# Value products of a token tile in one matmul run, and block outputs written into a dead input tile

## The chip, the cores and the metric

The kernel runs on one core of a Trainium2 chip. The metric is the device time of one execution in microseconds (us). Where several runs are shown, their median counts.

## The reference: what is computed

Two stages follow each other. The first is attention with 8 batches, 8 heads, 512 local and 32 global tokens and a head width of 64. A local token looks at the 32 tokens on either side of it and at the global tokens; a global token looks at all 544. The second is a two-layer network over the 4352 resulting rows of 512 numbers, with 2048 hidden units.

```
s_ll = scale * q_l @ k_l.T, masked to |i-j| <= 32;  s_lg = scale * q_l @ k_g.T
out_l = softmax([s_lg, s_ll]) @ [v_g, v_l]
out_g = softmax(scale * q_g @ [k_g, k_l].T) @ [v_g, v_l]
x = [out_g, out_l], one row of 512 for each token
h = x @ w_in;  g = h / (1 + exp(-h));  result = g @ w_out
```

The weights arrive in 64-bit floats and are decoded on the chip.

## The kernel before, in words

**Steps and tiles.** A step, numbered k from 0 to 127, handles 128 local tokens of one batch and two heads (u = 0, 1). Four steps (the index `pr`, 0 to 3, which stands for pairs of heads) make a token tile of 128 tokens by 512 columns. Four tiles (the index c, 0 to 3) make a batch. There are 32 such tiles, and two more hold the global rows of four batches each.

**A step.** `st_load` and `st_vload` fetch queries with keys (`raw`) and values (`vraw`). `st_scores` makes the scores of both heads in PSUM (`s`), and VectorE and ScalarE turn them into probabilities (`probs`). These have to be transposed into `pt`. For k under 24 TensorE transposes them (`t`), and ScalarE copies the result. From k = 24 on, GpSimd splits the words into halves (`st_halves`), a DMA writes them to DRAM (`st_away`), and a transposing DMA brings them back into `pt` (`st_back`). `st_turn` also lets GpSimd copy the columns of the global probabilities into `pt`. `st_out` then makes the value products: four matmuls in fp32, each appearing in the trace as two records. The values of 128 rows by 64 columns are the stationary operand, `pt` streams 128 or 160 columns, and the two heads use the two column halves of the array. One PSUM bank (`o`) takes the result of a step. ScalarE rounds it into `xh`, VectorE writes the remainder into `xl`, and a third instruction adds the partial sums of the global rows to `acc`.

**The first 28 steps** score with one fp32 matmul for each head. It uses 64 rows of the array, and each head writes a bank of its own. Later steps split their operands into high and low parts, and both heads share a bank.

**The network.** The 34 tiles are grouped into 12 blocks (`SIZES`), ten of three tiles and two of two. For a block `n` and a slice `f` of 128 hidden units (16 of them), `first_layer` makes 12 matmuls into `h` from `xh`, `xl` and the weights, ScalarE and VectorE turn that into `gh` and `gl`, and `second_layer` adds nine matmuls (three for each tile) to the banks `out`. After the last slice ScalarE copies these banks to tiles named `o`, two buffers in rotation, from which the results leave by DMA.

**The order of the work.** TensorE's order is that in which the program is written. Every part of a step gets a time in steps relative to its score (`DUE`, and `DMAT` from k = 24 on): the parts are sorted by it into one stream, and `fill` lets the stream advance a little after each piece of the network. So the attention steps of block n+1 are spread over the matmuls of block n. Before block 0 there is nothing to fill, and its twelve steps run alone. The queue of SyncE (SP) takes DMAs in the stream's order from k = 28 on. A scheduler orders the other engines.

**Buffers that matter.** `pt` has 3, `vraw` 4, `halves` 1, and the copies in DRAM (`planes`) 2. Outside the start, three PSUM banks rotate over scores, transposes and value products.

Of the kernel before, what the change touches and what calls it, by code (L numbers as in the profile page):

```python
# [16 lines left out]
ALU = mybir.AluOpType  # L17
# [19 lines left out]


SIZES = (3,) * 10 + (2, 2)
BUFS = dict(qk=2, raw=2, p=2, vraw=4, halves=1, pt=3)  # L40
ND = 28
KF = 24
GF = 3
# [3 lines left out]
FIRSTW = {2: 1, 3: 1, 4: 1, 5: 1, 6: 1, 7: 1, 8: 1, 9: 1, 10: 1, 11: 1}  # L47
JOINS, SPLITS = (9.0, 9.6, 10.2, 10.8, 11.4, 12.0), (12.1, 12.7)

FIRST = dict(load=(-1.2, -1.1, -1.0, 0.1), vload=(-0.9, 0.2, 0.3, 1.1), turn=(3.2, 4.0, 4.9, 5.8), out=(4.3, 5.2, 6.1, 7.0),  # L50
             gload=(1.2, 2.2, 3.2, 3.3), gscores=(3.4, 4.2, 5.1, 6.0), gsoft=(4.4, 6.2), gturn=(6.9, 8.0),
             late=8.5, then=7.3)

DUE = dict(load=-1.2, split=-0.5, vload=-0.6, turn=1.6, out=2.2)
DMAT = dict(vload=2.2, halves=0.7, away=1.05, turn=1.3, back=1.65, out=3.4)
HEAD = dict(load=-0.6, split=0.2, scores=0.8, soft=1.0, slot=0.3)
HEADS0, HEADS = (11, 1), (7, 2)
TURN1, TURN = (0.65, 1.5), (0.4, 1.5)
# [4 lines left out]
def attention_moe_kernel(ctx: ExitStack, tc: tile.TileContext, qk0_in, qk_in, v_in, gqk, wts, out):  # L63
    nc = tc.nc
# [3 lines left out]
    work = ctx.enter_context(tc.tile_pool(name="work", bufs=1))  # L68
    two = ctx.enter_context(tc.tile_pool(name="two", bufs=2))
    small = ctx.enter_context(tc.tile_pool(name="small", bufs=4))  # L70
    planes = ctx.enter_context(tc.tile_pool(name="planes", bufs=2, space=bass.MemoryType.DRAM))
    ps_att = ctx.enter_context(tc.tile_pool(name="ps_att", bufs=1, space=PSUM))
    ps_h = ctx.enter_context(tc.tile_pool(name="ps_h", bufs=2, space=PSUM))
    ps_out = ctx.enter_context(tc.tile_pool(name="ps_out", bufs=1, space=PSUM))
# [92 lines left out]
    def fetch_weights():  # L167
        i = w_next[0]
        w_next[0] += 1
        f, half = divmod(i, 2)  # L170
        if half and f >= SCRATCH:
            homes_ = [work.tile([P, QW + KW], I32, tag="qk", bufs=BUFS["qk"], name=f"raw_w{i}_{q}")[:, :DM] if f % 2
                      else two.tile([P, DM], I32, tag="o", name=f"raw_w{i}_{q}") for q in range(2)]
        else:
            taken.add(f + SCRATCH * half)
            homes_ = [scratch(f + SCRATCH * half, I32, f"raw_w{i}")]
        n = DM // len(homes_)
        w_raw.append([(raw, q * n, n) for q, raw in enumerate(homes_)])
        for raw, c0, n in w_raw[i]:
            hold(nc.sync.dma_start(out=raw, in_=wts[f, :, DM * half + c0 : DM * half + c0 + n].bitcast(I32)))  # L180
# [111 lines left out]
    tiles = {}  # L292
# [27 lines left out]
    def st_scores(k, b, c, pr):  # L320
        if k < ND:
            raw = tiles.pop(("raw", k))
        else:
            qk, klo = tiles.pop(("qk", k))
        if k < ND:
            ss = [attbank("s", f"s{k}_{u}")[:, :W] for u in range(2)]
            for u in range(2):
                rows = slice(D * u, D * (u + 1))
                nc.tensor.matmul(ss[u], raw[rows, P * u : P * (u + 1)], raw[rows, QW : QW + W], start=True, stop=True)  # L329
        else:  # L330
            s = attbank("s", f"s{k}")
            ss = [s[:, u * W : (u + 1) * W] for u in range(2)]
            for u in range(2):
                q, ks = qk[:, u * P : (u + 1) * P], slice(u * W, (u + 1) * W)
                nc.tensor.matmul(ss[u], q, qk[:, QW:][:, ks], start=True, stop=False)  # L335
                nc.tensor.matmul(ss[u], q, klo[:, ks], start=False, stop=True)  # L336
# [12 lines left out]
        nc.vector.tensor_scalar(out=p[:, 1, :W], in0=p[:, 1, :W], scalar1=st[:, 7:8], scalar2=None,  # L349
                                op0=ALU.mult)  # L350
        tiles["p", k] = p.rearrange("p u j -> p (u j)")
# [36 lines left out]
            src = pgu[SG * pr : SG * (pr + 1), :].rearrange("p (u q) -> p u q", u=2)  # L388
            nc.gpsimd.tensor_copy(out=pt[:SG, :, 1, P:], in_=src)

    def st_out(k, b, c, pr, t):
        n, i = block_of[t]
        xh, xl = xtiles(n)
        sl = slice(i * P, (i + 1) * P)
        vraw, pt = tiles.pop(("vraw", k)), tiles.pop(("pt", k))
        if k < NPR:
            tiles["late", k] = vraw
        o = attbank("o", f"o{k}")
        wide = P + SG
        for a in range(2):  # L400
            m = wide if (a == 0 or c == NC - 1) and k >= NPR else P
            for u in range(2):
                nc.tensor.matmul(o[D * u : D * (u + 1), :m], vraw[:, a, u, :], pt[:, u, a, :m], start=(a == 0),  # L403
                                 stop=(a == 1))
        nc.scalar.copy(out=xh[:, pr, sl], in_=o[:, :P])
        nc.vector.tensor_tensor(out=xl[:, pr, sl], in0=o[:, :P], in1=xh[:, pr, sl].bitcast(F32), op=ALU.subtract)  # L406
        if k >= NPR:
            gdst = acc[:, pr, SG * (b % 4) : SG * (b % 4 + 1)]
            if c == 0 and k >= NST:
                nc.vector.tensor_copy(out=gdst, in_=o[:, P:wide])  # L410
            else:
                nc.vector.tensor_tensor(out=gdst, in0=o[:, P:wide], in1=gdst, op=ALU.add)
# [30 lines left out]

    def xtiles(n):
        if n not in xblk:
            xblk[n] = tuple(two.tile([P, NPR, 3 * P], F32R, tag=f"x{j}", name=f"x{j}_{n}") for j in "hl")
        return xblk[n]


# [3 lines left out]
    def put(when, fn, *a):  # L453
        stream.append((when, fn, a))

    AHEAD = NPR
    for k, (t, b, c, pr) in enumerate(steps):
# [102 lines left out]
    def second_layer(n, f, gh, gl):  # L560
        if f == 0:
            outs[n] = [ps_out.tile([P, DM], F32, tag=f"out{i}", name=f"out{n}_{i}") for i in range(SIZES[n])]
        wh, wl = w_hi[f][:, DM:], w_lo[f][:, DM:]

        last = n + 1 == len(SIZES) and f == NF - 1
        for i in (reversed(range(SIZES[n])) if last else range(SIZES[n])):
            o = outs[n][i]
            sl = slice(i * P, (i + 1) * P)
            nc.tensor.matmul(o, gh[:, sl], wh, start=(f == 0), stop=False)  # L569
            nc.tensor.matmul(o, gh[:, sl], wl, start=False, stop=False)  # L570
            nc.tensor.matmul(o, gl[:, sl], wh, start=False, stop=(f == NF - 1))  # L571
# [103 lines left out]
```

## Time and profile before

| | |
|---|---|
| median of three runs | 1020.04 us (1017.97 to 1020.83) |
| the profiled execution | 1017.49 us |
| its span, first to last instruction | 1015.7 us |
| granted TensorE clock, mean | 0.989 |
| TensorE matmul busy | 990.8 us (98%) |
| VectorE, ScalarE, GpSimd busy | 632.2, 586.7, 236.6 us |

In the profile, PE is TensorE's matmuls, PEld its weight loads, DVE is VectorE, ACT is ScalarE, POOL is GpSimd and SP is SyncE. A row of the timeline gives the start, the duration, the engine, the line of the kernel, the operation, what is written from what, and the shapes. `128*64` means 128 rows and 64 columns of the array. Matmuls are pipelined, so their durations overlap: what a matmul costs is read from the distance between the starts of neighbours.

### The profile page before, as it was taken

How to read it: one execution, taken by the hardware profiler on the slowest of the kernel's cores; microseconds unless marked ns; L12 is line 12 of the kernel's file. 1: busy time of each engine (PE TensorE's matmuls, PEld its weight loads, DVE VectorE, ACT ScalarE, POOL GpSimd, SP SyncE). 2: the span in 40 equal slices, each digit the busy share in tenths (PEclk: the TensorE clock that was granted, in tenths of full speed). 3: DMA queues.
4: the chain of work that ended last, by engine and by line, in shares of the span. 5: the costliest groups of instructions: out<-in, count | busy, mean ns of one | idle time of the engine just before them, and what ended most of it. 6: DMA issues, size and time to landing. Idle time of an engine off the chain costs nothing.

```text
span 1015.7 us, 17864 instructions
## 1 busy us (share of the span) xinstructions
PE 990.8 (98%) x5792; PEld 838.9 (83%) x5792; DVE 632.2 (62%) x1977; ACT 586.7 (58%) x1549; POOL 236.6 (23%) x420
## 2 busy tenths in 40 slices
PE   7899899999999999999999999999999999999998
PEld 4567667888888888888888888888888888888896
DVE  4678874666776577755577667766677665543332
ACT  7788665565756655654566555665566555443332
POOL 2153432223222222211222212221222221110000
PEclk9799999999999999999999999999999999999999
DMA  8683525667665675544475567566766665432000
GB/s 302 205 289 130 158 84 146 163 161 179 187 167 152 176 172 151 166 116 121 119 176 164 145 188 173 145 171 161 172 148 169 158 171 141 121 93 63 1 22 21
DMA packets 177116, 151.05 MB, mean 149 GB/s; under 512 B 117376, under 2 KB 137344, under 8 KB 177024
## 3 DMA queue, kind: packets, MB, share of 16 engines
q1 hardware_dynamic: 172800, 142.32, 51.8%
q10 hardware_dynamic: 4224, 7.60, 2.2%
q8 instruction: 46, 0.75, 0.3%
q14 instruction: 46, 0.38, 0.1%
HBM read 86.44 MB, written 36.18 MB: 121 GB/s over the span
## 4 chain that ended last, share of the span: by engine, by line
PE 90%; DVE 4%; ACT 3%; issue 1%; POOL 0%; DVEq 0%; ACTq 0%; POOLq 0%
PE h L547 36%; PE out L569 13%; PE out L570 12%; PE out L571 12%; PE o L403 8%; PE s L335 2%; PE s L336 2%; DVE w L201 1%; PE s L329 1%; DVE raw_w L200 1%; PE gs L245 1%; PE t L377 1%; PE gt L283 1%; ACT w L198 1%; ACT w_hi L210 1%
## 5 line engine op out<-in xcount | busy, mean ns | idle before, releaser
L547 PE MATMUL h<-xh,w_hi 128*128 128x384 f32 (+1 forms) x768 | 255.8, 333 | 0.5 <-DVE st L340 0.5
L547 PE MATMUL h<-xl,w_hi 128*128 128x384 f32 (+1 forms) x768 | 251.7, 328 | 0.6 <-DVE xl L406 0.6
L547 PE MATMUL h<-xh,w_lo 128*128 128x384 f32 (+1 forms) x768 | 252.1, 328 | 0.0
L569 PE MATMUL out<-w_hi,gh 128*128 128x512 f32 x544 | 225.7, 415 | 0.5 <-ACT gh L556 0.4
L553 ACT ACTIVATE t<-h 128x384 f32<-128x384 f32 (+1 forms) x192 | 90.6, 472 | 221.0 <-PE h L547 203.5
L571 PE MATMUL out<-w_hi,gl 128*128 128x512 f32 x544 | 214.1, 394 | 3.8 <-DVE gl L557 3.8
L570 PE MATMUL out<-w_lo,gh 128*128 128x512 f32 x544 | 214.3, 394 | 0.0
L359 POOL COPY halves<-probs 128x512 uint16<-128x512 uint16 x208 | 141.3, 704 | 243.0 <-DVE probs L349 122.2
L554 DVE SCALAR_TENSOR_TENSOR t<-t,h 128x384 f32<-128x384 f32 (+1 forms) x192 | 101.8, 530 | 105.5 <-ACT t L553 104.2
L547 PEld LDWEIGHTS h<-xh,w_hi 128*128 128x128 f32 x768 | 145.1, 189 | 13.1 <-issue 6.2
L557 DVE TENSOR_TENSOR gl<-t,gh 128x384 fp32r<-128x384 f32 (+1 forms) x192 | 106.5, 555 | 77.3 <-PE out L571 64.8
L344 ACT ACTIVATE probs<-probs,st 128x224 f32<-128x224 f32 x244 | 116.2, 477 | 60.9 <-DVE st L340 59.3
L547 PEld LDWEIGHTS h<-xl,w_hi 128*128 128x128 f32 x768 | 145.2, 189 | 6.7 <-DVE xl L406 0.9
L547 PEld LDWEIGHTS h<-xh,w_lo 128*128 128x128 f32 x768 | 144.9, 189 | 0.0
L340 DVE CUSTOM_DVE_ANT_0 probs<-s,mask 128x224 f32<-128x224 f32 x244 | 86.7, 387 | 87.4 <-PE s L336 73.4
L556 ACT CAST gh<-t 128x384 fp32r<-128x384 f32 (+1 forms) x192 | 94.7, 493 | 59.3 <-DVE t L554 57.7
L569 PEld LDWEIGHTS out<-w_hi,gh 128*128 128x128 f32 x544 | 102.6, 189 | 31.1 <-issue 12.5
L571 PEld LDWEIGHTS out<-w_hi,gl 128*128 128x128 f32 x544 | 102.3, 188 | 28.5 <-DVE gl L557 5.4
L386 POOL COPY pt<-pgt 128x64 f32<-128x64 f32 x124 | 37.4, 302 | 370.9 <-PE o L403 292.5
L570 PEld LDWEIGHTS out<-w_lo,gh 128*128 128x128 f32 x544 | 103.0, 189 | 11.2
L403 PE MATMUL o<-pt,vraw 128*64 128x160 f32 x992 | 92.6, 307 | 4.9 <-issue 3.4
L403 PEld LDWEIGHTS o<-pt,vraw 128*64 128x64 f32 x992 | 60.2, 138 | 41.5 <-issue 33.1
(85 smaller groups left out, 1171.9 us busy)
## 6 DMA issues: line engine op xcount, KB each, us to landing
raw<-in_qk_dram SPq DMA_DIRECT2D x100, 352.0 KB, 3.4
away<-halves SPq DMA_DIRECT2D x104, 256.0 KB, 2.1
vraw<-in_v_dram SPq DMA_DIRECT2D x124, 128.0 KB, 3.1
raw_w<-in_wts_dram SPq DMA_DIRECT2D x24, 512.0 KB, 4.7
raw_g<-in_gqk_dram SPq DMA_DIRECT2D x32, 304.0 KB, 3.7
out_dram<-o ACTq DMA_DIRECT2D x28, 256.0 KB, 2.4
raw<-in_qk_dram SPq DMA_DIRECT2D x28, 240.0 KB, 3.1
raw_w<-in_wts_dram SPq DMA_DIRECT2D x16, 256.0 KB, 3.3
```

Source lines behind the costliest of these rows:

```text
L340: nc.vector.tensor_tensor_reduce(out=p[:, u, :W], in0=ss[u], in1=mask_of[c], scale=-SCALE, scalar=3.0e38, op0=ALU.add, op1=ALU.min, accum_ ...
L344: nc.scalar.activation(p[:, u, :W], p[:, u, :W], AF.Exp, bias=st[:, u : u + 1], scale=-1.0, accum_out=st[:, 2 + u : 3 + u])
L359: nc.gpsimd.tensor_copy(out=halves[:, :, u], in_=p[:, 2 * P * u : 2 * P * (u + 1)].bitcast(U16).rearrange("p (j h) -> p h j", h=2))
L403: nc.tensor.matmul(o[D * u : D * (u + 1), :m], vraw[:, a, u, :], pt[:, u, a, :m], start=(a == 0), stop=(a == 1))
L547: nc.tensor.matmul(h[:, :nt], wt, x[:, c, :nt], start=(i == 0), stop=(i == 3 * NCC - 1))
L553: nc.scalar.activation(t[:, :nt], h[:, :nt], AF.Tanh, scale=0.5)
L554: nc.vector.scalar_tensor_tensor(out=t[:, :nt], in0=t[:, :nt], scalar=1.0, in1=h[:, :nt], op0=ALU.add, op1=ALU.mult)
L556: nc.scalar.copy(out=gh[:, :nt], in_=t[:, :nt])
L557: nc.vector.tensor_tensor(out=gl[:, :nt], in0=t[:, :nt], in1=gh[:, :nt].bitcast(F32), op=ALU.subtract)
L569: nc.tensor.matmul(o, gh[:, sl], wh, start=(f == 0), stop=False)
L570: nc.tensor.matmul(o, gh[:, sl], wl, start=False, stop=False)
L571: nc.tensor.matmul(o, gl[:, sl], wh, start=False, stop=(f == NF - 1))
```

## The change: what it does

- `st_out` is called once for a tile instead of once for a step. It makes the value products of the tile's four steps one behind another, two steps in each of two PSUM banks. Each bank is then evicted with one ScalarE copy, one VectorE subtraction and one VectorE addition to `acc`, over twice the columns.
- Its time is 3.2 steps after the last of the four scores (2.2 for k under 24, and 7.0 on the stream's own scale for the first tile). Before, each step had its own at 3.4 (2.2).
- `pt` has 4 buffers and `planes` 3. The loads of values, the turns and the transposing DMAs of a tile's first steps get later times (`FIRST4`, `DMAT4`), so that they stand behind the run of the tile before.
- The scores of the first 28 steps use all 128 rows and one bank for both heads (`raw` is zero in the other head's rows).
- The `o` tiles go. The results of block n are copied into one tile that takes the place of the block's own `xh`, and leave from there. Two small weight staging buffers move to the tags `o` and `halves`, with one buffer each.

```
-BUFS = dict(qk=2, raw=2, p=2, vraw=4, halves=1, pt=3)
+BUFS = dict(qk=2, raw=2, p=2, vraw=4, halves=1, pt=4)
-FIRST = dict(load=(-1.2, -1.1, -1.0, 0.1), vload=(-0.9, 0.2, 0.3, 1.1), turn=(3.2, 4.0, 4.9, 5.8), out=(4.3, 5.2, 6.1, 7.0),
+FIRST = dict(load=(-1.2, -1.1, -1.0, 0.1), vload=(-0.9, 0.2, 0.3, 1.1), turn=(3.2, 4.0, 4.9, 5.8), out=7.0,
-DMAT = dict(vload=2.2, halves=0.7, away=1.05, turn=1.3, back=1.65, out=3.4)
+DMAT = dict(vload=1.5, halves=0.7, away=1.05, turn=1.3, back=1.65, out=3.2)
+FIRST4 = (dict(vload=1.25), dict(vload=0.3))
+DMAT4 = (dict(vload=2.25, turn=2.3, back=2.4),)
...
-            ss = [attbank("s", f"s{k}_{u}")[:, :W] for u in range(2)]
-                nc.tensor.matmul(ss[u], raw[rows, P * u : P * (u + 1)], raw[rows, QW : QW + W], start=True, stop=True)
+        s = attbank("s", f"s{k}")
+        ss = [s[:, u * W : (u + 1) * W] for u in range(2)]
+                nc.tensor.matmul(ss[u], raw[:, qs], raw[:, QW : QW + W], start=True, stop=True)
...
-    def st_out(k, b, c, pr, t):
+    def st_out(k0, b, c, t):
+        for pr in range(NPR):
+            k = k0 + pr
+            vraw, pt = tiles.pop(("vraw", k)), tiles.pop(("pt", k))
+            if pr % 2 == 0:
+                banks_.append(attbank("o", f"o{k}"))
+            o = banks_[-1][:, wide * (pr % 2) : wide * (pr % 2 + 1)]
...
+        for i, o in enumerate(banks_):
+            prs = slice(2 * i, 2 * i + 2)
+            o = o[:, : 2 * wide].rearrange("p (r q) -> p r q", r=2)
+            hi = xh[:, prs, sl]
+            nc.scalar.copy(out=hi, in_=o[:, :, :P])
+            nc.vector.tensor_tensor(out=xl[:, prs, sl], in0=o[:, :, :P], in1=hi.bitcast(F32), op=ALU.subtract)
+            if k0:
+                gdst = acc[:, prs, SG * (b % 4) : SG * (b % 4 + 1)]
...
-        put(at + due["out"], st_out, *a, t)
+        if pr == NPR - 1:
+            put(at + due["out"], st_out, k - pr, b, c, t)
...
+            done_ = work.tile([P, 3 * DM], F32, tag=f"xh{n % 2}", name=f"o{n}")
-                    sb = two.tile([P, DM], F32, tag="o", name=f"o{n}_{i}")
+                sb = done_[:, DM * i : DM * (i + 1)]
```

The first place is TensorE inside block 2 of the network, at the value products of steps 40 to 43. `o40` is the bank, `pt1` the transposed probabilities, `vraw40` the values, `out2_1` an output bank of block 2, `gs` the scores of global tokens. Before, step 40 stands alone:

```order
L570 MATMUL out2_1_3006<-w_lo4_900,gh2_4_3178 128x512
L571 MATMUL out2_1_3006<-w_hi4_899,gl2_4_3179 128x512
L403 MATMUL o40_3286<-pt1_127,vraw40_3203 64x160 x2
L403 MATMUL o40_3286<-pt1_127,vraw40_3203 64x128 x2
L569 MATMUL out2_2_3007<-w_hi4_899,gh2_4_3178 128x512
L570 MATMUL out2_2_3007<-w_lo4_900,gh2_4_3178 128x512
```

Now the four steps stand together:

```order
L252 MATMUL gs1_3_3_3381<-klo_g3_3_3343,qk_g3_3_3342 128x272
L408 MATMUL o40_3391<-pt0_126,vraw40_3096 64x160 x2
L408 MATMUL o40_3391<-pt0_126,vraw40_3096 64x128 x2
L408 MATMUL o40_3391<-pt1_127,vraw41_3121 64x160 x2
L408 MATMUL o40_3391<-pt1_127,vraw41_3121 64x128 x2
L408 MATMUL o42_3400<-pt2_128,vraw42_3207 64x160 x2
L408 MATMUL o42_3400<-pt2_128,vraw42_3207 64x128 x2
L408 MATMUL o42_3400<-pt3_129,vraw43_3279 64x160 x2
L408 MATMUL o42_3400<-pt3_129,vraw43_3279 64x128 x2
L583 MATMUL out2_1_2894<-w_hi8_1184,gh2_8_3309 128x512
```

Before, the steps 40 to 43 stood one by one in the pieces of slices 4, 5, 7 and 8 of block 2. The first three moved back to the fourth, in slice 8.

The second place is SP's queue at the same steps. `away` is the write of the halves to DRAM, the row with `DMA_TRANSPOSE` brings them back. Before:

```order
L364 DMA away40_3098<-halves40_3070 128x1024
L299 DMA raw42_3100<-in_qk_dram 128x704
L368 DMA_TRANSPOSE pt1_127<-away40_3098 128x4x256
L364 DMA away41_3191<-halves41_3143 128x1024
L299 DMA raw43_3193<-in_qk_dram 128x704
L307 DMA vraw40_3203<-in_v_dram 128x256
L368 DMA_TRANSPOSE pt2_128<-away41_3191 128x4x256
```

Now:

```order
L364 DMA away40_3000<-halves40_2960 128x1024
L302 DMA raw42_3002<-in_qk_dram 128x704
L364 DMA away41_3089<-halves41_3018 128x1024
L302 DMA raw43_3091<-in_qk_dram 128x704
L310 DMA vraw40_3096<-in_v_dram 128x256
L368 DMA_TRANSPOSE pt0_126<-away40_3000 128x4x256
L310 DMA vraw41_3121<-in_v_dram 128x256
L368 DMA_TRANSPOSE pt1_127<-away41_3089 128x4x256
L221 DMA raw_g3_2_3144<-in_gqk_dram 128x608
L364 DMA away42_3177<-halves42_3151 128x1024
L302 DMA raw44_3179<-in_qk_dram 128x704
```

The way back of step 40 moved behind the way out of step 41 and behind the load of the values of step 40; the load of `raw44` now follows two such pairs.

The third place is TensorE just ahead of block 0, where nothing else fills the engine. `t11` are the transposes of step 11, `h0_0` is the first matmul of the network. Before:

```order
L377 MATMUL t11_647<-ident_88,probs__118 128x128 x4
L245 MATMUL gs0_1_1_664<-raw_g1_1_607 64x272
L245 MATMUL gs1_1_1_667<-raw_g1_1_607 64x272
L403 MATMUL o11_670<-pt2_128,vraw11_555 64x160 x2
L403 MATMUL o11_670<-pt2_128,vraw11_555 64x128 x2
L329 MATMUL s13_0_685<-raw13_645 128x224
L329 MATMUL s13_1_686<-raw13_645 128x224
L547 MATMUL h0_0_702<-xh_0_233,w_hi0_618 128x384
```

Now:

```order
L377 MATMUL t11_596<-ident_88,probs__118 128x128 x4
L248 MATMUL gs0_1_1_611<-raw_g1_1_565 64x272
L248 MATMUL gs1_1_1_614<-raw_g1_1_565 64x272
L408 MATMUL o8_617<-pt0_126,vraw8_488 64x160 x2
L408 MATMUL o8_617<-pt0_126,vraw8_488 64x128 x2
L408 MATMUL o8_617<-pt1_127,vraw9_490 64x160 x2
L408 MATMUL o8_617<-pt1_127,vraw9_490 64x128 x2
L408 MATMUL o10_626<-pt2_128,vraw10_492 64x160 x2
L408 MATMUL o10_626<-pt2_128,vraw10_492 64x128 x2
L408 MATMUL o10_626<-pt3_129,vraw11_524 64x160 x2
L408 MATMUL o10_626<-pt3_129,vraw11_524 64x128 x2
L333 MATMUL s13_650<-raw13_594 128x224 x2
```

The value products of steps 8 to 10 moved behind the transposes of step 11, which hold the last probabilities that the tile needs.

More of the change, by code (lines that the diff above doesn't have):

```diff
@@ L70, in attention_moe_kernel @@
     small = ctx.enter_context(tc.tile_pool(name="small", bufs=4))
-    planes = ctx.enter_context(tc.tile_pool(name="planes", bufs=2, space=bass.MemoryType.DRAM))
+    planes = ctx.enter_context(tc.tile_pool(name="planes", bufs=3, space=bass.MemoryType.DRAM))
     ps_att = ctx.enter_context(tc.tile_pool(name="ps_att", bufs=1, space=PSUM))
@@ L172, in fetch_weights @@
             homes_ = [work.tile([P, QW + KW], I32, tag="qk", bufs=BUFS["qk"], name=f"raw_w{i}_{q}")[:, :DM] if f % 2
-                      else two.tile([P, DM], I32, tag="o", name=f"raw_w{i}_{q}") for q in range(2)]
+                      else work.tile([P, DM], I32, tag="halves" if q else "o", bufs=1, name=f"raw_w{i}_{q}")
+                      for q in range(2)]
         else:
@@ L324, in st_scores @@
             qk, klo = tiles.pop(("qk", k))
-        if k < ND:
-            ss = [attbank("s", f"s{k}_{u}")[:, :W] for u in range(2)]
[L327 to L336, printed above, removed]
+        s = attbank("s", f"s{k}")
+        ss = [s[:, u * W : (u + 1) * W] for u in range(2)]
+        for u in range(2):
+            qs, ks = slice(u * P, (u + 1) * P), slice(u * W, (u + 1) * W)
+            if k < ND:
+                nc.tensor.matmul(ss[u], raw[:, qs], raw[:, QW : QW + W], start=True, stop=True)
+            else:
+                nc.tensor.matmul(ss[u], qk[:, qs], qk[:, QW:][:, ks], start=True, stop=False)
+                nc.tensor.matmul(ss[u], qk[:, qs], klo[:, ks], start=False, stop=True)
         p = probs_tile(k)
@@ L394, in st_out @@
         sl = slice(i * P, (i + 1) * P)
[L395 to L398, printed above, removed]
         wide = P + SG
[L400 to L412, printed above, removed]
+        banks_ = []
+        for pr in range(NPR):
+            k = k0 + pr
+            vraw, pt = tiles.pop(("vraw", k)), tiles.pop(("pt", k))
+            if k < NPR:
+                tiles["late", k] = vraw
+            if pr % 2 == 0:
+                banks_.append(attbank("o", f"o{k}"))
+            o = banks_[-1][:, wide * (pr % 2) : wide * (pr % 2 + 1)]
+            for a in range(2):
+                m = wide if (a == 0 or c == NC - 1) and k >= NPR else P
+                for u in range(2):
+                    nc.tensor.matmul(o[D * u : D * (u + 1), :m], vraw[:, a, u, :], pt[:, u, a, :m], start=(a == 0),
+                                     stop=(a == 1))
+        for i, o in enumerate(banks_):
[6 more added lines that the diff above has]
+                gdst = acc[:, prs, SG * (b % 4) : SG * (b % 4 + 1)]
+                if c == 0:
+                    nc.vector.tensor_copy(out=gdst, in_=o[:, :, P:])
+                else:
+                    nc.vector.tensor_tensor(out=gdst, in0=o[:, :, P:], in1=gdst, op=ALU.add)
     def g_late():
@@ L445, in xtiles @@
         if n not in xblk:
-            xblk[n] = tuple(two.tile([P, NPR, 3 * P], F32R, tag=f"x{j}", name=f"x{j}_{n}") for j in "hl")
+            xblk[n] = tuple(work.tile([P, NPR, 3 * P], F32R, tag=f"x{j}{n % 2}", name=f"x{j}_{n}") for j in "hl")
         return xblk[n]
@@ L462, in attention_moe_kernel @@
             due.update(DMAT)
+            due.update(DMAT4[pr] if pr < len(DMAT4) else {})
+        elif k >= 2 * NPR:
+            due.update(FIRST4[pr] if pr < len(FIRST4) else {})
         if k < AHEAD:
-            due.update({part: FIRST[part][k] - k for part in ("load", "vload", "turn", "out")})
+            due.update({part: FIRST[part][k] - k for part in ("load", "vload", "turn")})
+            due["out"] = FIRST["out"] - k
         if k == AHEAD:
@@ L492, in attention_moe_kernel @@
             put(at + due["back"], st_back, *a)
-        put(at + due["out"], st_out, *a, t)
-        marks[t] = at + due["out"]
+        if pr == NPR - 1:
+            put(at + due["out"], st_out, k - pr, b, c, t)
+            marks[t] = at + due["out"]
         if j == NST - 1 and b % 4 == 3:
@@ L573, in second_layer @@
         if f == NF - 1:
+            done_ = work.tile([P, 3 * DM], F32, tag=f"xh{n % 2}", name=f"o{n}")
             for i in (reversed(range(SIZES[n])) if last else range(SIZES[n])):
                 o = outs[n][i]
-                if last and i == 0:
-                    sb = raws.tile([P, QW + KW], F32, tag="raw", name="o_last")[:, :DM]
-                else:
-                    sb = two.tile([P, DM], F32, tag="o", name=f"o{n}_{i}")
+                sb = done_[:, DM * i : DM * (i + 1)]
                 nc.scalar.activation(sb, o, AF.Copy, scale=0.5)
```

## Prediction

> **What bounds the kernel now.** I read the page's busy shares and chain first, then busy time by stage, then the waits of the matmul engine, and last its timeline around single value products. Share of the span and the chain that ended last:
>
> ```profile
> PE 990.8 (98%) x5792; PEld 838.9 (83%) x5792; DVE 632.2 (62%) x1977; ACT 586.7 (58%) x1549; POOL 236.6 (23%) x420
> PE 90%; DVE 4%; ACT 3%; issue 1%; POOL 0%; DVEq 0%; ACTq 0%; POOLq 0%
> ```
>
> By stage (stretch, its length, busy time and instructions of PE, PEld, DVE, ACT, POOL, clock, DMA share):
>
> ```profile
> 0.00:53.00 53.00, 42.10 (x251) 26.89 (x252) 28.79 (x134) 39.88 (x118) 12.20 (x41) 0.87 0.76 254
> 53.00:145.00 92.00, 83.12 (x450) 64.04 (x451) 76.26 (x201) 68.42 (x179) 39.28 (x38) 0.96 0.53 172
> 250.00:550.00 300.00, 300.00 (x1757) 261.15 (x1756) 199.22 (x617) 176.23 (x460) 69.35 (x129) 1.00 0.59 156
> ```
>
> The start (to 53 us) is shared by PE, ACT and latencies. Block 0 (to 145 us) has about 9 us in which PE idles. After that PE never rests, DVE is at 66% and ACT at 59%. From 145 us on the view of waits has one line for PE:
>
> ```profile
> PE s L335 <- DVE qk L318: 0.4, 1, 0.4
> ```
>
> So in those 870 us the kernel lasts as long as its matmul stream, and every nanosecond out of that stream comes off the time, as long as no new wait appears.
>
> **The price of a lone value product.** PE's timeline around one step with columns 160, 160, 128, 128, and around one of a batch's last tile, where all four have 160:
>
> ```profile
> 241.01 0.33 PE L547 MATMUL h<-xl,w_hi 128*128 128x384 f32 x1
> 241.19 0.34 PE L547 MATMUL h<-xh,w_lo 128*128 128x384 f32 x1
> 241.46 0.71 PE L403 MATMUL o<-pt,vraw 128*64 128x160 f32 x8
> 242.09 0.50 PE L569 MATMUL out<-w_hi,gh 128*128 128x512 f32 x1
> 242.43 0.40 PE L570 MATMUL out<-w_lo,gh 128*128 128x512 f32 x1
> ...
> 221.91 0.39 PE L571 MATMUL out<-w_hi,gl 128*128 128x512 f32 x1
> 222.23 0.76 PE L403 MATMUL o<-pt,vraw 128*64 128x160 f32 x8
> 222.93 0.50 PE L569 MATMUL out<-w_hi,gh 128*128 128x512 f32 x1
> 223.27 0.40 PE L570 MATMUL out<-w_lo,gh 128*128 128x512 f32 x1
> 223.51 0.40 PE L571 MATMUL out<-w_hi,gl 128*128 128x512 f32 x1
> ```
>
> Starts of neighbours give the costs: an `h` matmul 0.17 (241.19 - 241.01), an `out` matmul 0.23 to 0.24. Three distances are longer. From `h` into the value product it is 0.27 (0.10 more). The first `out` behind it lasts 0.34 to its successor (0.11 more). The run itself holds a third surplus, as its inside shows. The first row below stands when two records run, the next with four, then six; the last is a start, of the second pair:
>
> ```profile
> 241.46 0.36 PE L403 MATMUL o<-pt,vraw 128*64 128x160 f32 x2
> 241.46 0.49 PE L403 MATMUL o<-pt,vraw 128*64 128x160 f32 x4
> 241.46 0.60 PE L403 MATMUL o<-pt,vraw 128*64 128x160 f32 x6
> 241.64 0.53 PE L403 MATMUL o<-pt,vraw 128*64 128x160 f32 x6
> 318.26 0.60 PE L283 MATMUL gt<-ident,pg 128*128 128x128 f32 x4
> 318.69 0.27 PE L286 MATMUL gu<-ident,pg 128*32 128x128 f32 x1
> ```
>
> The two heads run at the same time, in pairs. The second pair ends 0.13 behind the first, the third and fourth (0.71) 0.11 each. Those are the streaming times: four transposes of 128 columns take 0.43, so 0.108 for 128 columns and 0.135 for 160. Only the first pair needs more (its successor starts 0.18 later, 0.05 over). A step inside a longer run should thus cost 2 x 0.135 + 2 x 0.108 = 0.49. The lone one occupies PE from 241.19 + 0.17 to 242.43 - 0.23, which is 0.84. In the last tile it is 0.90 (222.14 to 223.04) against 4 x 0.135 = 0.54. **Each step that joins another saves 0.35 us.**
>
> **The count.** Records of value products by stage, eight for a step:
>
> ```profile
> 0.00:53.00 53.00, 11.26 (x96) 7.61 (x96) 0.87 0.76 254
> 53.00:145.00 92.00, 8.23 (x80) 5.26 (x80) 0.96 0.53 172
> 145.00:914.00 769.00, 73.79 (x816) 47.89 (x816) 1.00 0.59 155
> ```
>
> That is 12, 10 and 102 steps, and the last 4 of the 128 follow after 914 us. Three of four steps lose their lone place: 0.75 x 106 = 79 joins after 145 us, 79 x 0.35 = **27.5 us**, all on the bound. Bounds: if the first pair of each joined step still pays its 0.05, 0.30 x 79 = 24; above, 28.
>
> **Block 0**: 7.5 joins, 2.6 us, while PE is busy 90% of the time. It idles behind DVE's decoding of weights, and DVE gets lighter too (below). I take 2.5; bounds 0 (DVE decides) and 6 (some of the 9 us of idling goes as well).
>
> **Scores of steps 14 to 27** (14 of them, in blocks 0 and 1) lose their 64-row form:
>
> ```profile
> 173.68 0.34 PE L547 MATMUL h<-xh,w_lo 128*128 128x384 f32 x1
> 173.95 0.65 PE L329 MATMUL s<-raw 64*128 64x224 f32 x4
> 174.53 0.71 PE L403 MATMUL o<-pt,vraw 128*64 128x160 f32 x8
> ```
>
> Now: 0.58, with 0.10 ahead and about 0.10 behind as above, 0.78. Afterwards four records one behind another, at 224/128 x 0.108 = 0.19 each, 0.76, without the surcharges. No row has this form in fp32; bounded by no surcharge and 0.10 for a first load, the 14 give -0.3 to +1.1. I take 0.
>
> **The start.** Nine joins (3.1 us of PE) against 14 scores of 0.76 for 0.58 (2.5 us), and the last tile's three other steps (3 x 0.49 = 1.5 us) now stand behind the last transposes, on the way to block 0. PE idles for 11 of the 53 us, so none of this passes in full. I take 0, bounds -3 and +3.
>
> **Evictions.** One instruction for two steps:
>
> ```profile
> L405 ACT CAST xh<-o 128x128 fp32r<-128x128 f32 x128 | 33.0, 258 | 17.4 <-PE o L403 15.4
> L406 DVE TENSOR_TENSOR xl<-o,xh 128x128 fp32r<-128x128 f32 x128 | 36.3, 284 | 10.2 <-ACT xh L405 9.3
> L412 DVE TENSOR_TENSOR acc<-o,acc 128x32 f32<-128x32 f32 x96 | 17.3, 180 | 0.0
> L553 ACT ACTIVATE t<-h 128x256 f32<-128x256 f32 x32 | 12.3, 384 | 48.2 <-PE h L547 48.0
> L557 DVE TENSOR_TENSOR gl<-t,gh 128x256 fp32r<-128x256 f32 x32 | 13.6, 426 | 20.2 <-PE out L571 19.4 <-ACT gh L556 0.8
> ```
>
> With the 256-column rows as the price, ACT pays 0.38 for 2 x 0.26 and DVE 0.43 for 2 x 0.28, and `acc` goes from two of 0.18 to one of about 0.21 (an estimate: 32 columns more at the slope between 128 and 256). Over 64 pairs that frees 9 us of ACT and 18 of DVE. After 145 us both were hidden, so this counts 0. The cover could go at a block's first matmul, which needs the last tile's `xh` and `xl`. From block 1 on, the program's order has at least nine `out` matmuls (2.1 us) between the last run and it, and the second bank's half is read another 6 x 0.17 = 1.0 later, against 0.38 + 0.43. Covered; without the cover it would be up to 0.8 us in each of ten blocks. Results that leave from the dead `xh` tile, a third copy in DRAM and the moved weight staging (as deep as before) change nothing in PE's stream: 0.
>
> **Can the run start in time?** One step's way, with SP's queue (away, back), and how many scores there are in 300 us (two such records for a step):
>
> ```profile
> 591.49 0.26 PE L335 MATMUL s<-qk 128*128 128x224 f32 x1
> 597.45 0.38 SPq L364 DMA_DIRECT2D away<-halves  x1
> 601.42 1.23 SPq L368 DMA_TRANSPOSE pt<-away  x1
> 613.24 0.71 PE L403 MATMUL o<-pt,vraw 128*64 128x160 f32 x8
> pt<-away SPq DMA_TRANSPOSE x104, 3.3
> 250.00:550.00 300.00, 19.52 (x78) 14.77 (x78) 1.00 0.59 156
> ```
>
> A step lasts 300/39 = 7.7 us. The probabilities are back at 601.4 + 3.3 = 604.7, and the product follows 8.5 us later. The tile's last step decides now; its product comes at 3.2 steps instead of 3.4, so 1.5 us earlier, and 7 us remain. The first two steps must wait for the run before them to free `pt`, but then have 3.8 and 2.6 steps (29 and 20 us). SP stands still until that run; behind it are two loads of values and two ways back (2 x 0.4 + 2 x 1.23 = 3.3 us, with a load's issue taken like that of the way out), then the way out of the third step, which was not ready earlier either (its halves come 6 us after its score, and the run stands 0.2 steps behind that score). The run takes two of the three rotating PSUM banks; the next but one user of the first of them comes 1.8 steps (14 us) later, long after 0.8 us of eviction. New waits: 0, bounded at 5 us (0.2 a tile).
>
> **Sum.** 27.5 + 2.5 + 0 + 0 + 0 = 30 us. Against the profiled execution (1017.49 us, its span of 1015.7 and 1.8 around it) that gives 987.5. The median of the runs is 2.55 above that execution, so I predict **990 us**.
>
> **Rivals.**
>
> *Weight loads in the run are not hidden.* If each pair paid what the first one pays (0.05 more), a joined step would cost 0.69, and the joins save 0.15: 87 x 0.15 = 13 us, 1007 us. Against it: pairs two to four of the lone run come at streaming speed, although each has weights of its own. Chance 6%. The Trainium skill, "TensorE: Matmul & The Clock Gate", in "Part 3: Packing small matmuls", says that a weight load overlaps with running matmuls only where the row group differs; all 128 rows are used here, so by it the loads would show in every pair. The rows of 0.13 and 0.11 speak against that, as far as four pairs go.
>
> *Slower: the run waits for its probabilities.* PE takes its work in order, so a late `pt` of one step stops everything, 26.5 times. Its place is SP's queue at the way back of a tile's last step. The gain is used up at 30/26.5 = 1.1 us a tile, so once the probabilities come 7 + 1.1 = 8.1 us later than now. At 9 us later it would be 26.5 x 2 - 30 = 23 us slower, 1043 us. For it: a single set of `pt`, and SP, GpSimd (its four copies into `pt`) and PE waiting for each other in a ring once a tile. Against it: 7 us is more than twice the way back. Chance 5%.
>
> *Part of the gain turns into waits* (bank rotation, block starts, a slower start), 1006 to 1017 us: 4%. That the joins do not happen is ruled out by the order of the program. No difference, 2%.
>
> **How the numbers follow.** The forecast has 83%. From 24 + 0 - 3 - 1.1 - 5 = 15 us up to 28 + 6 + 3 + 0.3 = 37 us of gain gives 983 to 1005; with a little for the offset between runs I take 981 to 1006. Within 0.3% (3 us) this kernel can't be told from itself. Faster: 0.83 + 0.06 + 0.04 = 0.93; the same 0.02; slower 0.05.
>
> **What would show it.** Right: value records in groups of 32 with 2.3 us from start to start of what follows; about 0.49 between the steps inside; PE's list of waits after block 0 still nearly empty; the start within 3 us of 53. Wrong: 0.69 between steps (loads), a gap ahead of each group with a DMA `pt<-away` as the releaser (the ring), or `h` waiting for `xl` at block starts.

## The result

The changed kernel takes 1029.68 us (median of five runs, 1025.17 to 1031.24) against 1019.24 us of the kernel before. The ratio is 1.0094, with a 95% interval of 1.0066 to 1.0121: slower by some 1%, clear of the noise, where 990 us had been forecast. The profiled execution took 1031.03 us, its span 1029.2 us.

### The profile after

The page's shares, and the chain that ended last:

```profile
PE 974.7 (95%) x5792; PEld 855.7 (83%) x5792; DVE 628.4 (61%) x1851; ACT 581.3 (56%) x1485; POOL 222.4 (22%) x421
PE 59%; DMA 9%; ACT 6%; DVE 6%; issue 4%; POOL 2%; SPq 1%; ACTq 0%; POOLq 0%; DVEq 0%
```

PE held 90% of the chain before and holds 59% now; DMA, which had no share, has 9%. By stage (stretch, its length, busy time and instructions of PE, PEld, DVE, ACT, POOL, clock, DMA share and rate):

```profile
0.00:53.00 53.00, 38.50 (x249) 29.63 (x250) 27.83 (x120) 39.34 (x113) 11.59 (x43) 0.94 0.77 247
53.00:145.00 92.00, 80.28 (x440) 67.38 (x439) 76.30 (x183) 64.25 (x163) 38.53 (x35) 0.98 0.54 173
165.00:905.00 740.00, 717.60 (x4232) 636.35 (x4231) 469.17 (x1404) 423.03 (x1073) 157.25 (x321) 0.99 0.61 156
```

The last stretch, blocks 1 to 9 without their edges, in the kernel before:

```profile
165.00:905.00 740.00, 739.62 (x4315) 639.38 (x4314) 482.46 (x1522) 431.99 (x1135) 174.08 (x326) 1.00 0.61 158
```

PE rested for 0.4 of these 740 us before, and rests for 22.4 now. It gets through 83 fewer matmuls, though each value product has become cheaper.

**The joins did pay.** One run of four steps in the timeline (the first two rows are the same run, cut after 16 and after 24 records), and then a run of a batch's last tile with its neighbours:

```profile
254.57 1.20 PE L408 MATMUL o<-pt,vraw 128*64 128x160 f32 x16
254.57 1.69 PE L408 MATMUL o<-pt,vraw 128*64 128x160 f32 x24
254.57 2.18 PE L408 MATMUL o<-pt,vraw 128*64 128x160 f32 x32
...
338.50 0.34 PE L561 MATMUL h<-xh,w_lo 128*128 128x384 f32 x1
338.77 2.39 PE L408 MATMUL o<-pt,vraw 128*64 128x160 f32 x32
341.10 0.50 PE L583 MATMUL out<-w_hi,gh 128*128 128x512 f32 x1
341.43 0.40 PE L584 MATMUL out<-w_lo,gh 128*128 128x512 f32 x1
```

From 16 to 24 to 32 records the run grows by 0.49 us a step. The last tile's run occupies PE from 338.67 to 341.20 (its neighbours' usual distances of 0.17 and 0.23 taken off), which is 2.53; 0.90 + 3 x 0.54 = 2.52 was to be expected.

**The waits are new.** The top of PE's list from 145 us on, where the kernel before had one row of 0.4 us (a row of such a list gives who waited for whom, us in total, times, and the longest):

```profile
PE s L335 <- DVE qk L321: 7.6, 10, 1.7
PE out L583 <- ACT gh L570: 5.7, 7, 1.8
PE s L335 <- ACT qk L319: 2.9, 1, 2.9
```

PE waits for the rounded queries and keys and their remainders (both in `qk`) and for the hidden units (`gh`). What ScalarE waits for in the whole execution, before and then after:

```profile
ACT qk L316 <- DMA raw<-in_qk_dram: 8.2, 10, 2.6
```

```profile
ACT qk L319 <- DMA raw<-in_qk_dram: 50.7, 27, 6.3
ACT qk_g L230 <- DMA raw_g<-in_gqk_dram: 26.0, 13, 4.1
```

And SP's queue at the value load, before and then after:

```profile
SPq L307 <- PE o L403: 27.5, 13, 5.3
```

```profile
SPq L310 <- PE o L408: 86.7, 41, 6.8
```

How these hang together shows in one stretch of the timeline, of which all rows of SP up to 590.37 and single rows of PE and ScalarE stand here (start, duration, engine; in brackets the idle time ahead and what ended it):

```profile
581.34 0.34 SPq L364 DMA_DIRECT2D away<-halves  x1
...
584.73 2.39 PE L408 MATMUL o<-pt,vraw 128*64 128x160 f32 x32
...
585.54 0.33 SPq L310 DMA_DIRECT2D vraw<-in_v_dram  x1
585.96 2.36 SPq L368 DMA_TRANSPOSE pt<-away  x1
588.41 0.52 SPq L310 DMA_DIRECT2D vraw<-in_v_dram  x1
589.03 1.23 SPq L368 DMA_TRANSPOSE pt<-away  x1
590.37 0.51 SPq L302 DMA_DIRECT2D raw<-in_qk_dram  x1
...
595.01 0.78 ACT L319 CAST qk<-raw 128x704 fp32r<-128x704 f32 x1 [2.91 <-DMA raw<-in_qk_dram]
...
597.11 0.50 ACT L570 CAST gh<-t 128x384 fp32r<-128x384 f32 x1
...
597.67 0.50 PE L583 MATMUL out<-w_hi,gh 128*128 128x512 f32 x1 [1.53 <-ACT gh L570]
```

SP has issued a way out at 581.34 and then stands before the value load, whose buffer the run of four has yet to read. The run starts at 584.73, the load goes at 585.54, and two pairs of value load and way back leave, 4.8 us of issuing. Only then, at 590.37, does the query load go. It lands 4.6 us later. ScalarE has stood 2.91 us at its rounding, with `gh` behind it in its queue, and PE then waits 1.53 us for `gh`.

**The clock adds to it.** The two stretches right behind that wait:

```profile
599.20:602.60 3.40, 3.40 (x12) 2.82 (x10) 1.82 (x8) 2.07 (x7) 0.44 (x1) 0.50 0.85 292
602.60:606.00 3.40, 3.40 (x19) 3.10 (x19) 2.21 (x5) 1.64 (x5) 1.17 (x2) 1.00 0.35 100
```

In the first PE is granted half its clock: 12 matmuls instead of 19, 1.7 us of work lost. That happens three times after 145 us in this kernel, and in the kernel before not once between 145 us and its last microseconds.

### The profile page after: what moved, and what is told of

It reads as the page before. It is cut to its first block, busy times and chain, and to the rows that moved or that the text cites. A ratio compares the mean times of both kernels' runs of the same rounds, so it can differ in the third digit from the quotient of the medians.

```text
span 1029.2 us, 17644 instructions
## 1 busy us (share of the span) xinstructions
PE 974.7 (95%) x5792; PEld 855.7 (83%) x5792; DVE 628.4 (61%) x1851; ACT 581.3 (56%) x1485; POOL 222.4 (22%) x421
## 4 chain that ended last, share of the span: by engine, by line
PE 59%; DMA 9%; ACT 6%; DVE 6%; issue 4%; POOL 2%; SPq 1%; ACTq 0%; POOLq 0%; DVEq 0%
PE h L561 25%; PE out L583 8%; PE out L585 8%; PE out L584 8%; DMA raw<-in_qk_dram 7%; PE o L408 4%; PE s L335 2%; ACT qk L319 2%; PE s L336 2%; ACT probs L344 1%; DMA away<-halves 1%; DVE klo L320 1%; DMA raw_g<-in_gqk_dram 1%; POOL halves L359 1%; DVE qk L321 1%
## 5 line engine op out<-in xcount | busy, mean ns | idle before, releaser
L359 POOL COPY halves<-probs 128x512 uint16<-128x512 uint16 x208 | 133.1, 666 | 476.1 <-DVE probs L349 266.8
L583 PE MATMUL out<-w_hi,gh 128*128 128x512 f32 x544 | 223.1, 410 | 8.5 <-ACT gh L570 8.1
L585 PE MATMUL out<-w_hi,gl 128*128 128x512 f32 x544 | 217.1, 399 | 5.1 <-DVE gl L571 4.7
L344 ACT ACTIVATE probs<-probs,st 128x224 f32<-128x224 f32 x244 | 115.7, 475 | 60.6 <-DVE st L340 59.7
L320 DVE TENSOR_TENSOR klo<-raw,qk 128x448 fp32r<-128x448 f32 x100 | 71.5, 715 | 70.2 <-ACT qk L319 68.6
L319 ACT CAST qk<-raw 128x704 fp32r<-128x704 f32 x100 | 77.5, 775 | 50.9 <-DMA raw<-in_qk_dram 50.7
L348 ACT ACTIVATE probs<-probs,st 128x224 f32<-128x224 f32 x122 | 58.6, 481 | 30.8 <-DVE st L347 26.8
```

What stands on the lines that cost most here:

```text
L319: nc.scalar.copy(out=qk, in_=raw)
L359: nc.gpsimd.tensor_copy(out=halves[:, :, u], in_=p[:, 2 * P * u : 2 * P * (u + 1)].bitcast(U16).rearrange("p (j h) -> p h j", h=2))
```

## The experiments

The theories: **A**, late query and key loads in SP's queue are what costs. (`raw` holds queries and keys of local tokens, `raw_g` those of global ones.) **B**, GpSimd's copies into `pt` stop at the run and hold up the halves. **C**, the bursts of evictions on ScalarE and VectorE make `gh` late. **D**, a side part of the change costs the time. The ratio is taken to the kernel before that ran beside it (1018.5 to 1019.2 us). The last two columns come from the one profiled execution: the time up to the first `h` of block 1, and from there to the first of block 10.

| kernel | time, us | ratio to before (95%) | start and block 0, us | blocks 1 to 9, us |
|---|---|---|---|---|
| before | 1019.24 | | 161.4 | 752.7 |
| after | 1029.68 | 1.0094 (1.0066 to 1.0121) | 163.3 | 765.2 |
| scores128 | 1016.82 | 0.9975 (0.9957 to 0.9992) | 159.6 | 754.1 |
| raw_late | 1029.14 | 1.0106 (1.0090 to 1.0123) | 159.8 | 765.4 |
| back_late | 1037.75 | 1.0192 (1.0164 to 1.0220) | 162.8 | 770.5 |
| raw_first | 1007.85 | 0.9882 (0.9845 to 0.9918) | 164.6 | 743.2 |
| run_early | 1004.74 | 0.9864 (0.9819 to 0.9910) | 167.9 | 741.2 |
| pairs | 1006.93 | 0.9888 (0.9870 to 0.9906) | 163.4 | 740.3 |
| pairs_all | 1001.10 | 0.9831 (0.9783 to 0.9879) | 157.8 | 739.4 |
| pairs_raw | 997.99 | 0.9788 (0.9757 to 0.9819) | 161.1 | 737.0 |
| four_a | 1006.41 | 0.9876 (0.9844 to 0.9908) | 159.2 | 747.5 |
| four_c | 999.69 | 0.9807 (0.9780 to 0.9834) | 159.0 | 738.2 |
| four_b | 994.63 | 0.9760 (0.9730 to 0.9790) | 157.6 | 733.7 |

**scores128: the scores' part alone, in the kernel before.**

```
-        if k < ND:
-            ss = [attbank("s", f"s{k}_{u}")[:, :W] for u in range(2)]
...
+        s = attbank("s", f"s{k}")
+        ss = [s[:, u * W : (u + 1) * W] for u in range(2)]
...
+                nc.tensor.matmul(ss[u], raw[:, qs], raw[:, QW : QW + W], start=True, stop=True)
```

> The kernel before with one part of the change alone: the scores of the first 28 steps use all 128 rows and one bank for both heads. Theory A and the prediction: within 3 us of the kernel before, 1016 to 1022, since the 14 of them in blocks 0 and 1 cost -0.3 to +1.1 us and the start moves by no more than 3. Theory D (side parts of the change cost the time): 1024 to 1030.

1.9 us below the kernel before that ran beside it (1018.7), so no loss comes from this side part. The results' new tile and the moved staging were not tried by themselves; raw_first and four_b below keep all of D's parts and run 11 and 24 us faster than the kernel before, so these don't carry the loss either.

**raw_late: later query loads alone, in the kernel before.**

```
             due.update(DMAT)
+            due.update(dict(load=-0.85) if k % NPR < 2 else {})
```

> The kernel before with one edit: the query and key loads of each tile's first two steps stand 0.35 steps (2.7 us) later in SP's queue, from step 24 on. Nothing else is changed, no run is joined. Theory A: the lead of these loads falls from 9.7 to about 7 us, as the changed kernel's (8.2 and 7.8), ScalarE waits for raw instead of 8 us some 30 or more, and TensorE waits for scores and gh: slower by 6 to 20 us, 1025 to 1040. If late loads are not what costs (theories B, C): 1016 to 1022, ScalarE waits and TensorE doesn't notice.

Slower by 10.4 us, as much as the whole change, with no run joined and no eviction moved. The stretch from 165 to 905 us shows PE idle where it had not been, and PE's list from 145 us on has one row:

```profile
165.00:905.00 740.00, 732.18 (x4245) 628.39 (x4244) 477.08 (x1504) 426.08 (x1120) 166.51 (x323) 1.00 0.60 156
```

```profile
PE s L335 <- DVE qk L318: 7.5, 12, 2.4
```

Two details were expected wrongly. ScalarE's wait for `raw` rose to 12.1 us only, not to 30: PE's own wait was for the remainders made from these loads. And the measured lead, from a load's issue to its score, fell to 8.9 us for a tile's first step and 8.3 for its second (medians), not to 7: the loads stand 2.7 us later in the order, but the scores slipped with them. The kernel has no slack of 2.7 us in these loads; by which engine's queue the lateness reaches PE differs.

**back_late: the stop taken away, the burst left.**

```
-DMAT4 = (dict(vload=2.25, turn=2.3, back=2.4),)
+DMAT4 = (dict(vload=3.45, turn=2.3, back=3.5), dict(vload=2.55, back=2.6))
```

> The changed kernel with one edit: the loads of values and the ways back of a tile's first two steps get later times (3.45 and 3.5 instead of 2.25 and 2.4 for the first, 2.55 and 2.6 instead of 1.5 and 1.65 for the second), so that the load of the next tile's first queries and keys and the way out of the third step stand ahead of them in SP's queue. SP then no longer stops at the run with those loads behind it. Theory A (SP's stop makes the query and key loads late, ScalarE's rounding of them stands ahead of gh in its queue, and TensorE waits for gh and for the scores): most of the 38 us of new waits go; ScalarE's wait for raw falls from 51 us to under 15 and for raw_g from 26 to under 10; time 998 us (990 to 1008). Theory B (GpSimd's copies into pt stop at the run and hold up the halves behind them): unchanged, since GpSimd's order is untouched: 1024 to 1032. Theory C (the order of ScalarE and VectorE itself, with evictions in bursts, makes gh late): 1020 to 1030, with the waits for gh as long as before.

All three theories missed: 1037.75 us, slower still. SP's wait for the run at the value load fell from 86.7 to 9.6 us, and that did not help. Between 145 us and the last microseconds half the clock was granted for 23.9 us, against 10.2 in the change, so some 7 of the 8 us that it is slower go with the clock. The timeline of SP:

```profile
571.28 0.38 SPq L310 DMA_DIRECT2D vraw<-in_v_dram  x1
571.72 1.23 SPq L368 DMA_TRANSPOSE pt<-away  x1
573.00 0.57 SPq L310 DMA_DIRECT2D vraw<-in_v_dram  x1
573.61 1.23 SPq L368 DMA_TRANSPOSE pt<-away  x1
574.89 0.58 SPq L310 DMA_DIRECT2D vraw<-in_v_dram  x1
575.87 1.25 SPq L368 DMA_TRANSPOSE pt<-away  x1
577.24 0.50 SPq L302 DMA_DIRECT2D raw<-in_qk_dram  x1
```

The load of the tile's first queries now stood ahead, but that of the second step stood behind three pairs, which take 6 us to issue. Only the step that came late had been exchanged: the median lead is 13.3 us for a tile's first step and 7.2 for its second, where the change has 8.2 and 7.8. So theory A had to be told otherwise: not the stop itself costs, but every query load that stands behind the stop or behind the burst of ways back that a run of four releases.

**raw_first: query loads ahead of stop and burst, the burst spread.** Runs of four and their time stay as in the change.

```
-DMAT = dict(vload=1.5, ... out=3.2)
+DMAT = dict(vload=1.9, ... out=3.2)
-DMAT4 = (dict(vload=2.25, turn=2.3, back=2.4),)
+DMAT4 = (dict(load=-1.85, vload=3.1, turn=2.3, back=3.15), dict(load=-2.05, vload=2.3, back=2.35),
+         dict(back=1.95), dict(vload=1.5))
```

> The changed kernel (runs of four) with other times for SP's queue alone: the query and key loads of a tile's first two steps earlier (1.85 and 2.05 steps ahead of their scores instead of 1.2), so that they stand ahead of the stop and of the burst of ways back that follows it, and that burst spread (values and ways back of the first three steps at 3.1, 3.3 and 3.9). The run with later values and ways back (1037.8 us) had only moved the lateness: its second step's load stood behind three pairs of value load and way back that SP issued in 6.4 us (570.84 to 577.24). Theory A in its new form (a query load behind SP's stop or behind the burst comes late, ScalarE stops at its rounding, gh and scores come late): leads of the first two steps' loads at 9 us or more, and the time falls by most of the 38 us: 1000 us (992 to 1012). Theory C (bursts of four steps' evictions on ScalarE and VectorE make gh late, whatever the loads do): 1018 to 1030.

1007.85 us: 21.8 below the change, by times of SP's queue alone. The leads of a tile's first two steps are 12.4 and 14.0 us. ScalarE's waits have fallen, to 12.3 and 9.2 us where the kernel before has 8.2 and 2.7:

```profile
ACT qk L319 <- DMA raw<-in_qk_dram: 12.3, 12, 2.6
ACT qk_g L230 <- DMA raw_g<-in_gqk_dram: 9.2, 7, 3.5
```

That speaks for A and against C as the main cause, since the evictions come in the same bursts, and against B, since GpSimd's copies wait for the run nearly as they did (101.7 us in all, 112.5 in the change). Blocks 1 to 9 became 9.5 us shorter than before, not the 26 of the forecast; what holds back the rest was not taken apart.

**run_early: one number, the run 0.6 steps earlier.**

```
-DMAT = dict(vload=1.5, halves=0.7, away=1.05, turn=1.3, back=1.65, out=3.2)
+DMAT = dict(vload=1.5, halves=0.7, away=1.05, turn=1.3, back=1.65, out=2.6)
```

> The changed kernel with one number changed: the run of four stands 2.6 steps after the tile's last score instead of 3.2. The probabilities wait 10 us (median) before the run, 7.5 at least, so 4.6 us can go. SP's stop at the next tile's first value load becomes 4.6 us shorter, the burst behind it stays as long. Theory A: the leads of the first two steps' loads rise by up to 4 us, ScalarE's wait for raw falls from 51 to about 20 us, 1008 us (998 to 1020). Theory C: evictions come in the same bursts, 1024 to 1034. If the way back is what decides (the slower rival of the prediction): slower than 1030, with waits of the run for pt.

1004.74 us, a little better than A had it. What ScalarE and SP wait for in it:

```profile
ACT qk L319 <- DMA raw<-in_qk_dram: 4.7, 6, 1.9
...
SPq L310 <- PE o L408: 18.0, 19, 6.1
```

The prediction had counted 7 us before the run as room for the probabilities. Taking 4.6 us of them away cut SP's stop for the run from 86.7 to 18.0 us. (The rows, and this kernel's last two columns in the table, are from an execution of 1011.45 us, the longest of its four.)

**pairs: runs of two, no stop.**

```
-DMAT = dict(vload=1.5, halves=0.7, away=1.05, turn=1.3, back=1.65, out=3.2)
-DMAT4 = (dict(vload=2.25, turn=2.3, back=2.4),)
+DMAT = dict(vload=2.2, halves=0.7, away=1.05, turn=1.3, back=1.65, out=3.4)
+DMAT4 = ()
...
+        if k >= KF and pr % 2:
+            put(at + due["out"], st_out, k - pr, b, c, t, (pr - 1, pr))
```

> The changed kernel with runs of two steps instead of four from step 24 on: each run fills one bank and stands 3.4 steps after its second score; loads of values and ways back have the times of the kernel before (2.2 and 1.65), and the four pt buffers let them go without a stop. Two of four steps join instead of three: 53 joins after 145 us at 0.35 = 18.5 us, and 2.5 in block 0, which keeps its runs of four. Theory A: no stop in SP's queue, so no new waits, 1019 - 21 = 998 us (992 to 1006), leads of the raw loads about 9.7 us as in the kernel before. Theory C (bursts of evictions): bursts of half the size leave about half the loss, 19 us, so 1012 to 1020.

1006.93 us, 9 above the expectation of A and 1 above its range. In blocks 1 to 9 it gained 12.4 of the 18.5 us; start and block 0, with their runs of four, were 2.0 longer than before instead of 2.5 shorter.

**pairs_all: runs of two from the first step.** As above without the condition on `k`, and with the times of before for the first tile (`out=(4.3, 5.2, 6.1, 7.0)`, `FIRST4 = ()`).

> The kernel with runs of two steps (1006.9 us), now from the first step on: the first 24 steps also make runs of two instead of four, at the times that the kernel before has for each second step. There the run of four holds up the start and block 0 (stalls of 14.6 us in block 0, 11.9 in the kernel before): the last transposes of a tile stand ahead of all its value products. Expected: start and block 0 together 2 to 4 us shorter, 1003 us (999 to 1008).

1001.10 us. Start and block 0 take 157.8 instead of 163.4 us, which is the difference of the medians too (5.8): runs of four cost that much there.

**The combinations.** Three put runs of two up to step 23 ahead of runs of four; the last takes runs of two throughout, with earlier query loads.

```
 four_a: out=2.9, the other queue times of raw_first
 four_b: out=2.6, vload=1.9, DMAT4 = (dict(load=-1.85, vload=2.8, turn=2.0, back=2.85),
                                      dict(load=-2.05, vload=2.0, back=2.05), dict(back=1.9), dict(vload=1.5))
 four_c: out=2.6, the other queue times of the change
 pairs_raw: pairs_all with DMAT = dict(load=-1.6, vload=2.2, ...)
```

> Runs of two steps up to step 23 (as in the kernel of 1001.1 us), runs of four from step 24 on, with the queue times of the run with the loads ahead (1007.85 us) and the run of four at 2.9 steps instead of 3.2. Theory A alone: start and block 0 as in the kernel of 1001.1 us (157.8 us instead of 164.6, so 6.8 off 1007.85), and the waits of 1.2 us inside runs shrink or stay: 1000 us (995 to 1005). If runs of four cost nothing beyond late loads, it should beat runs of two by up to one join more per tile, 26.5 x 0.35 = 9 us: 992. Theory C in a weak form (a run of four delays the steps behind it by its 2.3 us and its double evictions): no better than runs of two, 1000 to 1006.

> As the kernel beside it, with the run of four at 2.6 steps and the values and ways back of the first three steps 0.3 steps earlier. Theory A: 997 us (991 to 1004), since the stop is shorter and the loads stand ahead of it. If the way back decides: waits of the run for pt, over 1004.

> Runs of two up to step 23, then runs of four at 2.6 steps with all other queue times those of the changed kernel (the run of 1004.74 us with the start of the 1001.1 us one). The start and block 0 of 1004.74 took 167.9 us, those of 1001.1 us 157.8: 10 us less, so 995 us (991 to 1001) if start and steady state add up.

> The kernel with runs of two from the first step on (1001.1 us), with all query and key loads from step 24 on 1.6 steps ahead of their scores instead of 1.2 (3 us more). Theory A: ScalarE's wait for raw falls from 17 us to under 5, and of the 7 us of stalls that are left after 145 us (most of them scores waiting for rounded queries) some 4 go: 998 us (995 to 1001).

four_b, at 994.63 us, beats both kernels and is inside its range. PE's stretch in it:

```profile
165.00:905.00 740.00, 736.02 (x4435) 662.79 (x4434) 477.15 (x1444) 433.17 (x1104) 165.94 (x329) 1.00 0.61 159
```

Its 4435 matmuls stand against 4315 before and 4232 after the change. four_c is inside its range. four_a missed, and its trace says why:

```profile
PE gs L251 <- DVE acc L421: 9.9, 8, 2.2
...
268.98 0.29 PE L252 MATMUL gs<-klo_g,qk_g 128*128 128x272 f32 x1
269.58 0.37 ACT L414 CAST xh<-o 128x256 fp32r<-128x256 f32 x1
270.19 0.42 DVE L415 TENSOR_TENSOR xl<-o,xh 128x256 fp32r<-128x256 f32 x1
270.52 0.21 DVE L421 TENSOR_TENSOR acc<-o,acc 128x64 f32<-128x64 f32 x1
270.88 0.36 PE L251 MATMUL gs<-qk_g 128*128 128x272 f32 x1 [1.62 <-DVE acc L421]
```

At 2.9 steps the run stands right ahead of the two global scores, which take the next two PSUM banks in rotation. The second one gets the run's first bank and waits until `acc` has been read out of it: 9.9 us in eight places. At 2.6 that wait is 0.6 us. pairs_raw got its 998 us, but only in part as expected. ScalarE's wait for `raw` did not fall (20.2 us, 16.6 in pairs_all). PE's wait for the remainders is gone from 145 us on (2.5 us in pairs_all), and blocks 1 to 9 are 2.4 us shorter. The intervals of the two kernels overlap, so a gain from the earlier loads is likely there but not shown.

## Why the prediction was wrong, point by point

- **Price of a join, 0.35 us: right.** The steps inside a run take 0.49 us, the run of a last tile 2.53.
- **Rival "weight loads in the run are not hidden": refuted.** A step would have taken 0.69. By the Trainium skill's "TensorE: Matmul & The Clock Gate", "Part 3: Packing small matmuls", a weight load overlaps only where the row group differs; the rows of 0.49 us, with all 128 rows in use, do not agree.
- **Scores at 0: not contradicted** (scores128 is 1.9 us faster in all). **Start 0 and block 0 -2.5: wrong.** Together they came out 1.9 longer. That is one execution against one, but the kernels agree: with runs of four at the start five kernels took 162.8 to 167.9 us, with runs of two five took 157.6 to 161.1, and with single steps three took 159.6 to 161.4. So runs of four cost more there than the joins saved. That it is because they stand behind a tile's last transposes was not tried by itself.
- **Evictions hidden: not contradicted**, since raw_first and four_b gained with the same bursts. The rotating banks were safe at 3.2 steps (no such wait) and at 2.6 (0.6 us), but not between: at 2.9 they cost 9.9 us.
- **"Can the run start in time?", "New waits: 0, bounded at 5 us": the step that failed.** The question itself was answered rightly; no run waited for the way back (five waited for GpSimd's copies into `pt`, 1.7 us in all), and the slower rival named the right queue and the wrong transfer. The working said that SP "stands still until that run" and then counted what is behind it: two value loads, two ways back, and "the way out of the third step". The queries and keys of the next tile's first steps, which stand behind these pairs in the same queue, were left out, although the order of SP shown ahead of the prediction has `raw44` there. They had 9.7 us from issue to score (median of a tile's first steps, before) and 8.2 and 7.8 after. raw_late shows that this kernel has no such room to give: with leads of 8.9 and 8.3 us it lost 10.4 us. So where "New waits: 0" had been counted, PE rested for 22.4 of the 740 us shown above.
- **Size of the failure.** Blocks 1 to 9 were to get some 26 us shorter and got 12.5 longer. Of the difference, gaps of more than 0.25 us in PE's row of starts make 28.5 us, the three stretches at half clock 5.1, and some 5 are spread in smaller gaps.
- **Not settled:** how much of PE's wait goes through ScalarE's queue (rounding ahead of `gh`) and how much straight through late scores. That was read from the timeline; the order on ScalarE is the scheduler's, and no kernel here changed it alone. ScalarE's wait for `raw` by itself does not rank the kernels (20.2 us in four_b, the fastest, and 12.1 in raw_late), and neither does the lead (run_early has 10.0 and 8.2 us and is faster than raw_first). Nor is it shown why four_b keeps 19.0 us in blocks 1 to 9 and not 26; gaps above 0.25 us make 5.4 of the 7 that lack.

## What to carry to other kernels

When a step is moved or gathered, walk through every in-order queue that waits for it, and write down all that stands behind the wait, the loads for quite other work first; then compare the lead that each has with the lead it will have. A wait that a wider batch makes in a DMA queue can be shortened from three sides: issue the urgent loads ahead of it, spread the burst that follows, or start the batch as soon as its operands are there. A saving on the engine that bounds the kernel counts only while its feeders keep their slack: here putting half of the query loads 2.7 us later in their queue cost 10.4 us.

## What the runs showed of the hardware

- A wait of 1.5 to 3 us on TensorE can cost more than itself. In the changed kernel, half the clock was granted for 3.41 us from 251.0 and from 722.0 us on, just behind these two waits:

```profile
250.31 0.34 PE L335 MATMUL s<-qk 128*128 128x224 f32 x1 [2.86 <-ACT qk L319]
...
721.78 0.59 PE L583 MATMUL out<-w_hi,gh 128*128 128x512 f32 x1 [1.84 <-ACT gh L570]
```

  The Trainium skill's "TensorE: Matmul & The Clock Gate", "Part 1: The HAM clock gate", puts the fall to half clock after an idle window of about 3.4 us; the length of the slow stretch agrees, but here gaps shorter than that window were enough. The rows are the 3.41 us up to each of the three falls, and a stretch that no fall followed:

```profile
247.62:251.03 3.41, 0.72 (x6) 0.75 (x7) 2.19 (x3) 1.97 (x3) 1.85 (x2) 1.00 0.04 15
595.79:599.20 3.41, 1.78 (x9) 0.97 (x9) 2.19 (x6) 3.17 (x9) 1.00 (x2) 0.99 0.72 165
718.62:722.03 3.41, 1.57 (x9) 1.25 (x8) 2.83 (x11) 2.15 (x8) 0.00 (x0) 1.00 0.65 124
186.15:189.56 3.41, 1.67 (x10) 1.22 (x9) 1.60 (x3) 1.78 (x4) 1.54 (x3) 1.00 0.78 159
```

  PE idled 2.7, 1.6 and 1.8 us ahead of the falls, and 1.7 us in the last row. So in this kernel about half of such a stretch idle can be enough; where the limit lies exactly is not shown.
- A transposing DMA costs 1.23 us of its queue's issuing time, against 0.33 to 0.58 for the plain ones (rows of the change and of back_late; one transposing DMA of the change took 2.36): three pairs of a value load and a way back hold up what stands behind them for 6 us, without any wait.
